# First w_gate chunk issued from the ScalarE queue beside the x tiles; parameter transpose moved into the gate/up work of block 0

## Chip, cores and metric

The kernel runs on one core of a Trainium2 chip. The metric is the device time of one execution in microseconds (us), a median over several runs. The profile's span is shorter than that time by about 1.8 us; all instants below are counted from the span's start.

## The reference

A layer norm of x (2048 rows of 512) feeds two branches that are added to x: a diagonal state-space model over 2048 steps, and a gated feed-forward layer.

```python
xn = _layernorm(x, axis=-1)
return x + _A_ref(xn, Lambda_re, Lambda_im, B_re, B_im, C_re, C_im, log_dt, Dskip) \
         + (_gelu(xn @ w_gate) * (xn @ w_up)) @ w_down      # w_gate, w_up: 512 x 1376
```

## The kernel before

Rows are handled in four blocks of 512. For each block TensorE does the gate and up products (GU), the product of the state-space input matrix with xn (BU), and the down product plus state output (DN). VectorE does the layer norms, the scans and the gelu products; ScalarE does most of the emptying of PSUM, where TensorE's results are written (PS in the profile lines). Every operation is recorded with an estimated duration, its reads and its writes. A list scheduler then picks the order of instructions on VectorE, ScalarE and GpSimd; TensorE and SyncE keep the order of recording. So a small edit can change the order on other engines.

The start of the kernel is what matters here. Cuts are marked.

```python
for j in range(4):
    ld_x0(j)                                  # four x tiles of block 0, SyncE queue
ld_w(WG, WGc, ins["B_w_gate"], 0)             # first chunks: 384 columns each, 384 KB
ld_w(WU, WUc, ins["B_w_up"], 0)
ld_w(WG, WGc, ins["B_w_gate"], 1)
ld_w(WU, WUc, ins["B_w_up"], 1)
for q, nm in enumerate(("A_log_dt", "A_Lambda_re", "A_Lambda_im")):
    S.dma(...PROW..., 1024, ..., queue="scalar")      # three loads of 1 KB, ScalarE queue
# ... cut ...
ACT(lambda e: e.activation(SCR.ap, HALF.ap[:, 0:1], ACTF.Sqrt), 200, [HALF, IOTJ], [SCR], "sqrt0")  # pulls in the Sqrt table
# ... cut: params() transposes the 12 x 128 parameters on TensorE, copies them on VectorE, and computes exp(log_dt) ...

def GU_first(fts, early, single):             # gate/up of block 0, F tiles 0..4; early = 0..2
    # ... cut: mm(ft, u, j0, j1) = 4 matmuls for x tiles j0..j1 (u = 0 gate, 1 up); evac = gelu + copy (ACT), product (V) ...
    for u in range(2):
        for ft in early:
            mm(ft, u, 0, 1)                   # x tile 0
            if single and u == 0 and ft == 1:
                TR0(1, "A")                   # transpose x tile 1, copy it to SBUF on ScalarE
    for ft in early:
        for u in range(2):
            mm(ft, u, 1, 2)                   # x tile 1
        evac(ft, 0)
    late = [ft for ft in fts if ft not in early]
    mm(late[0], 0, 0, 2)
    TR0(2, "V")                               # x tile 2, copied on VectorE
    TR0(3, "A")                               # x tile 3, copied on ScalarE
    for ft in late[1:]:
        mm(ft, 0, 0, 2)
    for ft in late:
        mm(ft, 1, 0, 2)
        evac(ft, 0)
    for ft in fts:                            # the "second half": x tiles 2 and 3
        for u in range(2):
            mm(ft, u, 2, 4)
        evac(ft, 1)

# recording order
PE(fwarm, ...)            # 11 matmuls of 128x512 on zeros, to get TensorE up to speed
LN(0, [0], True)          # layer norm of x tile 0; True: its square root is on ScalarE
TR0(0, "V")
fill(4)
params()
LN(0, [1], True, [GATE["bnag"]])
LN(0, [2, 3], True, [GATE["evT"]])
load_B()
GU_first(range(5), range(3), True)
# ... cut: sine tables, BU(0), the scan of block 0, blocks 1 to 3 ...
```

Of the kernel before, what the change touches and what calls it, by code (L numbers as in the profile page):

```python
# [10 lines left out]
ACTF = mybir.ActivationFunctionType  # L11
# [5 lines left out]
LAT = lambda d, op: SYNC_LAT if d.kind == "dma" or d.eng != op.eng else (0.0 if d.eng == "tensor" else SELF_LAT)  # L17
# [4 lines left out]
class Buf:  # L22
    __slots__ = ("name", "space", "lo", "hi", "ap")

    def __init__(self, name, space, lo, hi, ap=None):
        self.name, self.space, self.lo, self.hi, self.ap = name, space, lo, hi, ap
# [34 lines left out]

class Op:
    __slots__ = ("id", "eng", "fn", "dur", "deps", "kind", "reads", "writes", "start", "finish",
                 "sem", "val", "users", "tag", "issue")

    def __init__(self, id_, eng, fn, dur, kind, reads, writes, tag):
        self.id, self.eng, self.fn, self.dur, self.kind = id_, eng, fn, float(dur), kind
        self.reads, self.writes, self.tag = reads, writes, tag
        self.deps, self.users = [], []
        self.start = self.finish = None  # L70
        self.sem = None
        self.val = None
        self.issue = DMA_ISSUE


class Sched:
# [134 lines left out]
    def _forward(self, prio):  # L211
        ops = self.ops
        free_at = {e: 0.0 for e in ENGINES}
        dma_pipe = 0.0
        ndeps = {op.id: len(op.deps) for op in ops}
        ready = {e: [] for e in ENGINES}
        queue = {e: [op for op in ops if op.eng == e] for e in INORDER}
        qpos = {e: 0 for e in INORDER}
        for op in ops:
            if ndeps[op.id] == 0 and op.eng not in INORDER:  # L220
                ready[op.eng].append(op)
        order = {e: [] for e in ENGINES}
        nleft = len(ops)

        def rdy_time(op):
            return max([d.finish + LAT(d, op) for d in op.deps], default=0.0)

        while nleft:
            best = None
            for e in ENGINES:  # L230
                if e in INORDER:
                    if qpos[e] >= len(queue[e]):
                        continue
                    op = queue[e][qpos[e]]
                    if ndeps[op.id] != 0:
                        continue
                    st = max(free_at[e], rdy_time(op))
                else:
                    if not ready[e]:
                        continue  # L240
                    cands = [(max(free_at[e], rdy_time(op)), op) for op in ready[e]]
                    st0 = min(c[0] for c in cands)
                    stb, b = min(cands, key=lambda c: (prio[c[1].id], c[1].id))
                    if stb <= st0 + 150.0:
                        st, op = stb, b
                    else:
                        limit = max(stb, prio[b.id])
                        fill = [c for c in cands if c[1] is not b and
                                c[0] + (c[1].issue if c[1].kind == "dma" else c[1].dur) <= limit]
                        if fill:  # L250
                            f0 = min(c[0] for c in fill)
                            fill = [c for c in fill if c[0] <= f0 + 150.0]
                            st, op = min(fill, key=lambda c: (prio[c[1].id], c[1].id))
                        else:
                            st, op = stb, b
                if best is None or st < best[0]:
                    best = (st, op)
            st, op = best
            e = op.eng
            if e in INORDER:  # L260
                qpos[e] += 1
            else:
                ready[e].remove(op)
            op.start = st
            if op.kind == "dma":
                free_at[e] = st + op.issue
                xfer = op.dur - 2000.0
                t0 = max(st, dma_pipe)
                dma_pipe = t0 + xfer
                op.finish = t0 + xfer + 2000.0  # L270
            else:
                op.finish = st + op.dur
                free_at[e] = op.finish
            order[e].append(op)
            nleft -= 1
            for u in op.users:
                ndeps[u.id] -= 1
                if ndeps[u.id] == 0 and u.eng not in INORDER:
                    ready[u.eng].append(u)
        return order, max(op.finish for op in ops)  # L280
# [74 lines left out]
def d_dve_tt2x(n): return 100.0 + 0.52 * n  # L355
# [8 lines left out]
def build(nc, ins, out):  # L364
    with ExitStack() as es:
# [11 lines left out]
        WG = A.alloc("WG", [KD, F], BF16)  # L377
# [3 lines left out]
        WGc = [Buf("WGc%d" % i, "sbx", 10 * i, 10 * i + 1) for i in range(3)]  # L381
# [24 lines left out]
        HALF = A.alloc("HALF", [4], F32)  # L406
# [37 lines left out]
        IOTJ = A.alloc("IOTJ", [512], I32, at=OUTB_all.lo)  # L444
# [14 lines left out]
        def ld_w(W, Wc, src, ci, queue="sync"):  # L459
            f0, f1 = FCH[ci]  # L460
            return S.dma(lambda e: e.dma_start(W.ap[:, :, f0:f1], src[:, f0:f1].rearrange("(k p) f -> p k f", p=128)),  # L461
                         512 * (f1 - f0) * 2, writes=[Wc[ci]], tag="ld_w", queue=queue)

        def ld_x0(j):
            S.dma(lambda e, j=j: e.dma_start(X[j].ap, x2[128 * j:128 * (j + 1), :]), 128 * 1024, writes=[X[j]], tag="ld_x0")  # L465
        for j in range(4):
            ld_x0(j)
        ld_w(WG, WGc, ins["B_w_gate"], 0)
        ld_w(WU, WUc, ins["B_w_up"], 0)
        ld_w(WG, WGc, ins["B_w_gate"], 1)  # L470
        ld_w(WU, WUc, ins["B_w_up"], 1)
# [29 lines left out]
        ACT = lambda fn, dur, r, w, tag="", after=(): S.op("scalar", fn, dur, r, w, tag, after)  # L501
# [9 lines left out]
        V(lambda e: e.tensor_scalar(IDN.ap, IOT.ap, 0.0, None, ALU.is_equal), d_dve_ts4x(128), [IOT], [IDN], "ident")  # L511
        POOL(lambda e: e.iota(IOTJ.ap, [[1, 512]], base=0, channel_multiplier=0), 600, [], [IOTJ], "iotj")
        SCR = A.alloc("SCR", [1], F32)
        ACT(lambda e: e.activation(SCR.ap, HALF.ap[:, 0:1], ACTF.Sqrt), 200, [HALF, IOTJ], [SCR], "sqrt0")
        rstate = {"n": 0}

        def next_bank():
# [189 lines left out]
        def GU_first(fts, early, single):  # L707
            banks = [{ft: next_bank() for ft in fts} for h in range(2)]

            def mm(ft, u, j0, j1):  # L710
                W, Wc = ((WG, WGc), (WU, WUc))[u]
                h, q0 = j0 // 2, 256 * u + 128 * (j0 % 2)
                bank = banks[h][ft]

                def f(e):
                    ins_ = None
                    for dk in range(KD):
                        ins_ = e.matmul(PS[bank][:, q0:q0 + 128 * (j1 - j0)], W.ap[:, dk, 128 * ft:128 * (ft + 1)],  # L718
                                        XNT[0].ap[:, dk, 128 * j0:128 * j1], start=(dk == 0), stop=(dk == KD - 1))
                    return ins_  # L720
                PE(f, d_pe([128 * (j1 - j0)] * 4), [Wc[wchunk(ft)]] + XT0[j0:j1], [BANK[bank]], "GU0")

            def evac(ft, h):
                bank, c0 = banks[h][ft], 256 * h
                GATE["nh"] = kk = (GATE["nh"] + 1) % 3
                GATE["last_gelu"] = ACT(lambda e: e.activation(GG[kk].ap[:, 0:256], PS[bank][:, 0:256], ACTF.Gelu_apprx_tanh),
                                        d_act(256), [BANK[bank]], [GG[kk]], "gelu")
                ACT(lambda e: e.activation(UPB[kk].ap[:, 0:256], PS[bank][:, 256:512], ACTF.Copy),
                    d_act(256), [BANK[bank]], [UPB[kk]], "evU")
                V(lambda e: e.tensor_tensor(HTt[0][ft].ap[:, c0:c0 + 256], GG[kk].ap[:, 0:256], UPB[kk].ap[:, 0:256], ALU.mult),  # L730
                  d_dve_tt2x(256), [GG[kk], UPB[kk]], [HTt[0][ft]], "hmul")

            for u in range(2):
                for ft in early:
                    mm(ft, u, 0, 1)
                    if single and u == 0 and ft == 1:
                        TR0(1, "A")
            for ft in early:
                for u in range(2):
                    mm(ft, u, 1, 2)  # L740
# [3 lines that stand above are left out]
            TR0(2, "V")  # L744
            TR0(3, "A")
# [5 lines that stand above are left out]
            for ft in fts:  # L751
# [3 lines that stand above are left out]
# [95 lines left out]
        LN(0, [0], True)  # L850
        TR0(0, "V")
        fill(4)
        params()
        LN(0, [1], True, [GATE["bnag"]])
        LN(0, [2, 3], True, [GATE["evT"]])
        load_B()
# [85 lines left out]
```

## Time and profile before

| | before |
|---|---|
| median of 3 runs at first (6 runs later) | 182.26 us (182.19) |
| span of the profiled run, its time | 180.7 us, 182.48 us |
| matmul busy | 174.4 us, 97% |
| w_gate chunk 0: issued, landed | 2.66, 6.6 |
| w_up chunk 0: issued, landed | 3.13, 8.2 |
| BU of block 0 begins (first weight load) | 16.74 |

Lines of the page of before: span, busy time by engine, and the chain of work that ended last, by engine and by line.

```profile
span 180.7 us, 2411 instructions
...
PE 174.4 (97%) x865; PEld 84.2 (47%) x880; DVE 156.7 (87%) x270; ACT 93.9 (52%) x170; POOL 9.7 (5%) x20
...
PE 93%; DMA 3%; SPq 1%; issue 1%; DVE 0%; DVEq 0%
PE PS L767 37%; PE PS L802 36%; PE PS L655 15%; PE PS L718 5%; DMA arena<-in_B_w_up_dram 3%; SPq L465 1%; DVE arena L818 0%; PE PS L630 0%; SPq L461 0%; DVEq L331 0%
```

TensorE is busy nearly all the time, and the chain is matmuls but for a few per cent at the start. L767 is GU, L802 is DN, L655 is BU, L718 is the gate/up work of block 0 and L630 the x transposes. Next, all waits of TensorE in before: engine, line, what it waited for, us in total, times, longest.

```profile
PE PS L839 <- DVE arena L509: 1.0, 1, 1.0
PE PS L718 <- DVE arena L609: 0.7, 1, 0.7
PE PS L718 <- DMA arena<-in_B_w_up_dram: 0.6, 1, 0.6
PE PS L630 <- DVE arena L609: 0.2, 1, 0.2
```

All four lie in the first 8.3 us. Everything after is an unbroken stream of matmuls, so any gain must come from starting that stream earlier and keeping it whole. The 0.7 us wait, which ends at 6.63, is put down to VectorE's L609, but the copy of x tile 0 that these products need ended at 6.04 (L638, 5.62 + 0.42), and the weight loads ahead of them list 0.80 us for w_gate, which landed at 6.6. The timeline of before for that stretch (start, us, engine, line, operation, output and input, count, then the idle time ahead of it and what ended it; SPq and ACTq are DMA issues):

```profile
1.67 1.28 ACT L514 ACT_TABLE_LOAD   x1 [1.67 <-POOL arena L508]
...
2.66 0.43 SPq L461 DMA_DIRECT2D arena<-in_B_w_gate_dram  x1
...
2.83 0.69 DVE L596 BATCH_NORM_STATS2 arena<-arena 128x6 f32<-128x512 bf16 x1 [0.95 <-DMA arena<-in_A_x_dram]
...
3.13 0.51 SPq L461 DMA_DIRECT2D arena<-in_B_w_up_dram  x1
...
3.86 0.30 ACT L600 ACTIVATE arena<-arena 128x1 bf16<-128x1 bf16 x1 [0.70 <-DVE arena L597]
...
5.19 0.40 PE L630 MATMUL PS<-arena 128*128 128x128 bf16 x4 [0.16 <-DVE arena L609]
...
6.63 0.62 PE L718 MATMUL PS<-arena 128*128 128x128 bf16 x8 [0.71 <-DVE arena L609]
...
8.27 2.62 PE L718 MATMUL PS<-arena 128*128 128x128 bf16 x40 [0.57 <-DMA arena<-in_B_w_up_dram]
...
9.93 0.38 ACT L726 ACTIVATE arena<-PS 128x256 bf16<-128x256 f32 x1
...
11.17 5.84 PE L718 MATMUL PS<-arena 128*128 128x256 bf16 x52
11.37 0.60 ACT L636 ACTIVATE arena<-PS 128x512 bf16<-128x512 bf16 x1 [0.23 <-PE PS L630]
...
16.74 3.23 PEld L655 LDWEIGHTS PS<-arena 128*128 128x128 bf16 x16
```

TensorE: x transpose at 5.19, gate products at 6.63, then a wait for w_up until 8.27. ScalarE: Sqrt table load at 1.67, first layer-norm activation at 3.86, first gelu at 9.93, copy of x tile 3 at 11.37. The start of the second half is not a line of its own, as the 52 matmuls at 11.17 run on without a gap; 12 of them at 0.107 us put it at about 12.45.

The data rate of all DMAs in before, in forty slices of 0.3 us:

```profile
GB/s 0 0 0 0 0 24 208 236 208 252 253 311 259 79 79 125 282 328 346 348 315 294 256 270 270 250 312 294 311 372 393 382 382 386 382 386 382 373 327 256
```

After the x tiles there is a hole of 79 GB/s (3.9 to 4.5 us).

### The profile page before, as it was taken

Reading aid. Unit: us, or ns where it says so; the run is one execution under the profiler, and the core shown is the slowest. Engines: PE = TensorE matmul, PEld = TensorE weight load, DVE = VectorE, ACT = ScalarE, POOL = GpSimd, SP = SyncE. Lnnn points to the kernel's source line nnn. Section 1 sums busy time; section 2 is a strip of 40 time slices with the busy share of each in tenths; the row PEclk is TensorE's granted clock in tenths of the full one; section 3 lists DMA queues with packets and bytes.
Section 4 is the critical chain, followed back from the end, with each engine's and each line's share of the span. In section 5 each row is a group of like instructions: output and inputs, shape, how many; then the busy total and the mean of one; then the engine's idle time right before and its main releaser. Section 6 shows DMA issues by size and latency. Waiting matters only on the chain.

```text
span 180.7 us, 2411 instructions
## 1 busy us (share of the span) xinstructions
PE 174.4 (97%) x865; PEld 84.2 (47%) x880; DVE 156.7 (87%) x270; ACT 93.9 (52%) x170; POOL 9.7 (5%) x20
## 2 busy tenths in 40 slices
PE   7699999999999999999999999999999999999993
PEld 3497444444444444444444444444444444444441
DVE  4779996998989989988999999999989999998111
ACT  4497999876666899002667793000667701700000
POOL 2200112042000000200000000000000000000000
PEclk9999999999999999999999999999999999999999
DMA  5999925999000000002410000000000000003100
GB/s 127 293 326 176 317 46 113 173 314 252 1 0 4 0 0 0 0 31 89 89 29 0 2 0 4 29 29 29 29 0 0 4 0 0 0 0 116 62 29 29
DMA packets 24067, 12.38 MB, mean 68 GB/s; under 512 B 15384, under 2 KB 24056, under 8 KB 24056
## 3 DMA queue, kind: packets, MB, share of 16 engines
q1 hardware_dynamic: 24032, 12.23, 27.5%
q8 instruction: 7, 0.11, 0.3%
q14 instruction: 4, 0.03, 0.1%
q10 hardware_dynamic: 24, 0.00, 0.0%
HBM read 6.46 MB, written 2.10 MB: 47 GB/s over the span
## 4 chain that ended last, share of the span: by engine, by line
PE 93%; DMA 3%; SPq 1%; issue 1%; DVE 0%; DVEq 0%
PE PS L767 37%; PE PS L802 36%; PE PS L655 15%; PE PS L718 5%; DMA arena<-in_B_w_up_dram 3%; SPq L465 1%; DVE arena L818 0%; PE PS L630 0%; SPq L461 0%; DVEq L331 0%
## 5 line engine op out<-in xcount | busy, mean ns | idle before, releaser
L767 PE MATMUL PS<-arena 128*128 128x512 bf16 (+1 forms) x308 | 67.8, 379 | 0.2
L802 PE MATMUL PS<-arena 128*128 128x512 bf16 (+1 forms) x297 | 65.8, 379 | 0.4
L767 PEld LDWEIGHTS PS<-arena 128*128 128x128 bf16 (+1 forms) x312 | 31.4, 100 | 36.1
L779 ACT ACTIVATE arena<-PS 128x512 bf16<-128x512 f32 (+1 forms) x39 | 23.5, 603 | 46.2 <-PE PS L767 36.8
L802 PEld LDWEIGHTS PS<-arena 128*128 128x128 bf16 (+1 forms) x304 | 29.7, 98 | 36.0
L688 DVE TENSOR_TENSOR_SCAN arena<-arena 128x512 bf16<-128x512 f32 x32 | 38.9, 1255 | 0.9 <-POOL arena L536 0.9
L655 PE MATMUL PS<-arena 128*128 128x512 bf16 x124 | 27.7, 379 | 0.2
L782 ACT ACTIVATE arena<-PS 128x512 bf16<-128x512 f32 (+1 forms) x39 | 23.5, 602 | 7.2 <-PE PS L767 7.1
L818 DVE TENSOR_TENSOR arena<-PS,arena 128x512 bf16<-128x512 f32 x16 | 10.6, 681 | 10.7 <-PE PS L802 10.7
L655 PEld LDWEIGHTS PS<-arena 128*128 128x128 bf16 x128 | 12.5, 98 | 14.8
L659 ACT ACTIVATE arena<-PS 128x512 bf16<-128x512 f32 x32 | 17.9, 592 | 2.7 <-PE PS L655 2.6
L784 DVE TENSOR_TENSOR arena<-arena 128x512 bf16<-128x512 bf16 (+1 forms) x39 | 15.5, 414 | 3.6 <-ACT arena L782 3.3
L596 DVE BATCH_NORM_STATS2 arena<-arena 128x6 f32<-128x512 bf16 x16 | 10.3, 682 | 1.4 <-DMA arena<-in_A_x_dram 1.3
L718 PE MATMUL PS<-arena 128*128 128x256 bf16 (+1 forms) x104 | 9.5, 248 | 1.3 <-DVE arena L609 0.7
L794 ACT ACTIVATE PS<-arena 128x512 f32<-128x512 bf16 x16 | 9.4, 602 | 0.7
L677 DVE TENSOR_TENSOR arena<-arena 128x4096 bf16<-128x4096 bf16 (+1 forms) x5 | 9.3, 1856 | 0.0
L675 DVE TENSOR_TENSOR arena<-arena 128x4096 bf16<-128x4096 bf16 (+1 forms) x5 | 9.3, 1855 | 0.0
L700 DVE TENSOR_TENSOR arena<-arena 128x4096 bf16<-128x4096 bf16 x4 | 9.1, 2287 | 0.0
L701 DVE TENSOR_TENSOR arena<-arena 128x4096 bf16<-128x4096 bf16 x4 | 9.1, 2284 | 0.0
L718 PEld LDWEIGHTS PS<-arena 128*128 128x128 bf16 x104 | 8.1, 98 | 2.1 <-DMA arena<-in_B_w_gate_dram 0.8
L609 DVE TENSOR_SCALAR arena<-arena 128x512 bf16<-128x512 bf16 x16 | 5.9, 409 | 0.4
L572 DVE SCALAR_TENSOR_TENSOR arena<-arena 128x512 bf16<-128x512 bf16 x8 | 5.6, 747 | 0.7 <-ACT arena L569 0.7
(81 smaller groups left out, 89.4 us busy)
## 6 DMA issues: line engine op xcount, KB each, us to landing
out_dram<-arena SPq DMA_DIRECT2D x16, 128.0 KB, 1.7
arena<-in_A_x_dram SPq DMA_DIRECT2D x3, 512.0 KB, 7.6
arena<-in_B_w_down_dram SPq DMA_DIRECT2D x1, 1280.0 KB, 7.0
arena<-in_A_x_dram SPq DMA_DIRECT2D x4, 128.0 KB, 2.2
arena<-in_B_w_gate_dram SPq DMA_DIRECT2D x1, 512.0 KB, 5.9
arena<-in_B_w_up_dram SPq DMA_DIRECT2D x1, 512.0 KB, 6.8
arena<-in_B_w_gate_dram SPq DMA_DIRECT2D x1, 480.0 KB, 4.2
arena<-in_B_w_up_dram SPq DMA_DIRECT2D x1, 480.0 KB, 5.1
```

What stands on the lines that cost most here:

```text
L596: V(lambda e, tt=tt: e.bn_stats(ST[tt].ap, X[tt].ap), d_dve_1x(512), [X[tt]], [ST[tt]], "bnst", after)
L655: ins_ = e.matmul(PS[bank][:, :], BBT[c][dk].ap[:, 128 * s:128 * (s + 1)], XNT[b].ap[:, dk, :], start=(dk == 0), stop=(dk == KD - 1))
L659: ACT(lambda e, bank=bank, k3=k3, s=s, c=c: e.activation(SSc[k3][s][c].ap, PS[bank][:, :], ACTF.Copy), d_act(512), [BANK[bank]], [SSc[k3][ ...
L688: V(lambda e, g=g, rb=rb, init=init: e.tensor_tensor_scan(g.ap, rb, g.ap, init, ALU.mult, ALU.add), d_dve_scan(512), [g, PA[RRr]] + ([CARc ...
L718: ins_ = e.matmul(PS[bank][:, q0:q0 + 128 * (j1 - j0)], W.ap[:, dk, 128 * ft:128 * (ft + 1)], XNT[0].ap[:, dk, 128 * j0:128 * j1], start=( ...
L767: ins_ = e.matmul(PS[bank][0:m, c0:c1], W.ap[:, dk, 128 * ft:128 * ft + m], XNT[b].ap[:, dk, c0:c1], start=(dk == 0), stop=(dk == KD - 1))
L779: GATE["last_gelu"] = ACT(lambda e, bg=bg, kk=kk, m=m: e.activation(GG[kk].ap[0:m, :], PS[bg][0:m, :], ACTF.Gelu_apprx_tanh), d_act(512), ...
L782: ACT(lambda e, bu=bu, kk=kk, m=m: e.activation(UPB[kk].ap[0:m, :], PS[bu][0:m, :], ACTF.Copy), d_act(512), [BANK[bu]], [UPB[kk]], "evU")
L784: V(lambda e, kk=kk, m=m, ft=ft, k2=k2: e.tensor_tensor(HTt[k2][ft].ap[0:m, :], GG[kk].ap[0:m, :], UPB[kk].ap[0:m, :], ALU.mult), d_dve_tt ...
L794: ACT(lambda e: e.activation(PS[bank][:, :], X[tt].ap, ACTF.Copy), d_act(512), [X[tt]], [BANK[bank]], "seed")
L802: ins_ = e.matmul(PS[bank][:, :], l_[:, 128 * j:128 * (j + 1)], r_, start=False, stop=last and n == len(ops) - 1, skip_group_check=True)
L818: V(lambda e: e.tensor_tensor(OUTB[ko].ap, PS[bank][:, :], XD[tt].ap, ALU.add), d_dve_1x(512), [BANK[bank], XD[tt]], [OUTB[ko]], "evO")
```

## The change

The intent is to have the first weights arrive sooner, and to keep the parameter transpose from stalling TensorE once its last load sits behind w_gate on ScalarE's queue. `nb` is a "not before" time in the scheduler's model (ns), used only to place an operation in the order of its engine. The table load is thereby put after the DMA issues, and no longer waits for an iota.

```diff
-        ld_w(WG, WGc, ins["B_w_gate"], 0)
+        ld_w(WG, WGc, ins["B_w_gate"], 0, "scalar").nb = 900.0
@@
-        ACT(..., ACTF.Sqrt), 200, [HALF, IOTJ], [SCR], "sqrt0")
+        ACT(..., ACTF.Sqrt), 200, [HALF], [SCR], "sqrt0").nb = 1900.0
@@ rdy_time
-            return max([d.finish + LAT(d, op) for d in op.deps], default=0.0)
+            return max([d.finish + LAT(d, op) for d in op.deps] + [op.nb])
@@ GU_first, between the products of x tile 0 and those of x tile 1
+            params()
@@ recording order
         fill(4)
-        params()
```

(The field `nb` in the class of operations is cut.) Instruction orders that change: ScalarE issues log_dt, Lambda_re, w_gate, Lambda_im and only then loads the Sqrt table; and the scheduler puts one more gelu ahead of the copy of x tile 3. VectorE and GpSimd change in small places.

More of the change, by code (lines that the diff above doesn't have):

```diff
@@ L63 @@
     __slots__ = ("id", "eng", "fn", "dur", "deps", "kind", "reads", "writes", "start", "finish",
-                 "sem", "val", "users", "tag", "issue")
+                 "sem", "val", "users", "tag", "issue", "nb")
     def __init__(self, id_, eng, fn, dur, kind, reads, writes, tag):
@@ L73, in __init__ @@
         self.issue = DMA_ISSUE
+        self.nb = 0.0
 class Sched:
@@ L513, in build @@
         SCR = A.alloc("SCR", [1], F32)
-        ACT(lambda e: e.activation(SCR.ap, HALF.ap[:, 0:1], ACTF.Sqrt), 200, [HALF, IOTJ], [SCR], "sqrt0")
+        ACT(lambda e: e.activation(SCR.ap, HALF.ap[:, 0:1], ACTF.Sqrt), 200, [HALF], [SCR], "sqrt0").nb = 1900.0
         rstate = {"n": 0}
```

## The prediction

> **What bounds the kernel now.** TensorE. The profiled span is 180.7 us, matmuls are busy 174.4 us (97%), the granted clock is full. In the list of waits TensorE waits four times, all before 8.3 us: 1.0 us for the first memset, 0.2 and 0.7 us for layer-norm tiles, 0.6 us for w_up. In the timeline there is no gap over 0.1 us from 8.27 to 177.7 us, so time = start of the unbroken stream + fixed matmul work. The chain of waits agrees: x issues, the w_up chunk (issued 3.13, landed 8.22), then only matmuls.
>
> **What the change does.** (1) The first w_gate chunk (384 KB), issued from SyncE at 2.66 us, landing 3.9 us later, is issued from ScalarE behind two tiny loads that end at 1.58 us. w_up and all behind it on SyncE move up by its issue, 0.47 us. The data rate has a hole now (3.9 to 4.5 us, 80 to 125 GB/s against 250 to 380 around it), which this fills. The Trainium skill, "DMA: Bandwidth & Descriptors", section "Issuing engines are not separate DMA queues", says that such DMAs run on the same 16 engines and interleave, saving only issue time; so I expect no more bandwidth. Estimate: w_gate lands at 5.3 to 5.9 (was 6.6), w_up at 6.7 to 7.3 (was 8.2). (2) The parameter transpose (0.18 us) leaves the gap at 5.74 and goes behind the first up matmuls, about 8.0 us; its copy on VectorE ran only at 7.96, so little is lost. (3) The Sqrt table load (1.28 us) now sits behind four DMA issues on ScalarE: starts near 2.4 instead of 1.67, so the first layer-norm activation goes from 3.86 to about 4.0.
>
> **On the critical path.** First transpose 5.2 to 5.35; its copy done 6.1 to 6.25; gate matmuls start there instead of 6.63; second x transpose waits for its layer-norm tile, about 6.75; third gate tile ends near 7.4; w_up is there. So the stream starts near 7.4, not 8.27: 0.8 us gained. It isn't all kept. The second half of block 0 needs the copy of x tile 3 by ScalarE. Its gelu chain starts at 9.93 because of the layer norm of tiles 2 and 3, which the change doesn't speed up, and the new order puts one more gelu ahead of that copy. Five evacuations at 0.27 us and a 0.60 us copy end near 12.0 us; the second half starts at about 12.45 now (11.17 + 12 x 0.107). So TensorE idles some 0.4 us there, and about 0.4 us is left. Later slack carries it: the first BU matmul is at 16.8 now, its B_re transpose landed at 15.9 and moves up too.
>
> **Prediction.** 181.85 us, range 181.2 to 182.4 (runs of before scatter by 0.7). Faster by over 2%: 0.5%; within 2%: 99%; slower: 0.5%.
>
> **What would show it.** The w_up wait disappears; the 128-column gate/up matmuls run unbroken from near 7.4; a new TensorE wait of 0.2 to 0.5 us near 11.5 to 12 us, released by the ScalarE copy of x tile 3; BU of block 0 starts 0.3 to 0.5 us earlier, everything later is shifted alike; matmul busy time is unchanged.
>
> **What would make it wrong.** w_gate traffic interleaves with x tiles 0 and 1 and delays the first layer norm: no gain or slightly slower. Or the issue on ScalarE takes longer than 0.5 us and pushes the first layer norm beyond 4.1 us. Or the copy of tile 3 isn't the limit and 0.8 us is kept. None reaches 2% (3.6 us): the start-up idle at stake is 1.5 us.

## The result

| | before | after |
|---|---|---|
| median (range), 6 runs each | 182.19 (181.78 to 182.46) | 182.30 (182.25 to 182.75) |
| ratio, 95% interval | | 1.0012 (0.9995 to 1.0028) |
| span and time of the profiled run | 180.7, 182.48 | 180.8, 182.60 |
| w_gate chunk 0 landed | 6.6 | 5.8 |
| w_up chunk 0 landed | 8.2 | 7.35 |
| BU of block 0 begins | 16.74 | 16.84 |

Ratios are the mean time of one kernel's runs over that of the other's of the same rounds, so not quite the ratio of the medians. The change moved the time by less than the comparison can tell from nothing.

The page of after (span, busy, chain by engine):

```profile
span 180.8 us, 2410 instructions
...
PE 175.3 (97%) x865; PEld 84.5 (47%) x880; DVE 156.8 (87%) x270; ACT 93.8 (52%) x170; POOL 9.8 (5%) x20
...
PE 94%; ACT 2%; DVE 2%; issue 1%; DVEq 0%
```

The 2% of ScalarE and 2% of VectorE in the chain are new; DMA has left it. TensorE's waits in after:

```profile
PE PS L841 <- DVE arena L510: 1.0, 1, 1.0
PE PS L719 <- DVE arena L606: 0.4, 1, 0.4
PE PS L719 <- ACT arena L637: 0.3, 1, 0.3
```

The wait for w_up is gone, as intended. A wait for ScalarE's L637 has come in: that is the copy of x tile 3. The timeline of after:

```profile
1.60 0.43 ACTq L462 DMA_DIRECT2D arena<-in_B_w_gate_dram  x1
...
2.51 1.28 ACT L515 ACT_TABLE_LOAD   x1 [2.51 <-issue]
2.65 0.43 SPq L462 DMA_DIRECT2D arena<-in_B_w_up_dram  x1
...
2.94 0.69 DVE L597 BATCH_NORM_STATS2 arena<-arena 128x6 f32<-128x512 bf16 x1 [1.20 <-DMA arena<-in_A_x_dram]
...
4.09 0.30 ACT L601 ACTIVATE arena<-arena 128x1 bf16<-128x1 bf16 x1
...
5.66 0.46 PE L631 MATMUL PS<-arena 128*128 128x128 bf16 x4
...
7.46 1.06 PE L719 MATMUL PS<-arena 128*128 128x128 bf16 x16
...
8.45 0.18 PE L531 MATMUL PS<-arena 12*128 12x12 bf16 x1
...
10.46 0.38 ACT L727 ACTIVATE arena<-PS 128x256 bf16<-128x256 f32 x1
...
11.80 0.64 ACT L637 ACTIVATE arena<-PS 128x512 bf16<-128x512 bf16 x1
...
12.59 4.53 PE L719 MATMUL PS<-arena 128*128 128x256 bf16 x40 [0.32 <-ACT arena L637]
...
16.84 3.23 PEld L656 LDWEIGHTS PS<-arena 128*128 128x128 bf16 x16
```

The loads are issued and land earlier. The up products of x tile 0 begin at 7.69 rather than 8.27. (The line at 7.46 begins with four gate products, 0.056 us apart, which before ran at 7.31, ahead of its wait.) But the first gelu is at 10.46 instead of 9.93. Behind it come five evacuation steps and the copy at 11.80, and TensorE stops for it until 12.59. BU begins 0.1 us later than before. The remaining kernel costs the same: span minus the start of BU is 163.95 and 163.94 us in the two profiles, and the same within 0.03 us in all fourteen. So the start of BU tells all.

The starts of single matmuls in the two traces show where the gain goes. The up products begin 0.58 us earlier (8.27 to 7.69). The parameter transpose takes 0.21 of that: 0.26 us pass from the product ahead of it (8.30) to the one behind it (8.56), where 0.056 is the pace. So the 256-column products begin 0.37 us earlier (11.17 to 10.80). The stop for the copy takes 0.48: 0.59 us pass between two products 0.107 us apart in the stream. (The 0.32 us listed is less, because it counts from the modelled end of the last matmul.) The second half so begins 0.11 us later (12.48 to 12.59), and BU with it.

The data rate in after:

```profile
GB/s 0 0 0 0 0 24 154 254 159 261 102 60 215 369 364 365 377 363 359 378 361 330 298 307 276 287 331 345 386 386 382 386 376 379 372 376 325 246 105 184
```

The hole isn't filled. It has moved forward, to 3.0 to 3.6 us, and the x tiles' landing went from a median of 2.2 to 3.3 us after their issue. The packets in the traces show how: w_gate, issued at 1.60, sends its first packet at 2.87, and from 3.3 to 3.6 us the x tiles (1024 B packets of SyncE's queue) move 3 GB/s and w_gate (768 B packets of ScalarE's) 56. The last packet of the x tiles starts at 5.76 instead of 4.02. Only tile 0 is urgent, and it came at 2.94 against 2.83.

### The profile page after: what moved, and what is told of

Read it like the earlier page. It is cut to its first block, busy times and chain, and to the rows that moved or that the text cites. A ratio compares the mean times of both kernels' runs of the same rounds, so it can differ in the third digit from the quotient of the medians.

```text
span 180.8 us, 2410 instructions
## 1 busy us (share of the span) xinstructions
PE 175.3 (97%) x865; PEld 84.5 (47%) x880; DVE 156.8 (87%) x270; ACT 93.8 (52%) x170; POOL 9.8 (5%) x20
## 4 chain that ended last, share of the span: by engine, by line
PE 94%; ACT 2%; DVE 2%; issue 1%; DVEq 0%
PE PS L769 37%; PE PS L804 36%; PE PS L656 15%; PE PS L841 3%; PE PS L719 3%; ACT L727 1%; DVE arena L597 1%; ACT arena L727 1%; DVE arena L820 0%; ACT arena L729 0%; ACT arena L637 0%; DVE arena L639 0%; DVE arena L610 0%; ACT arena L601 0%; PE PS L631 0%
## 5 line engine op out<-in xcount | busy, mean ns | idle before, releaser
L656 PE MATMUL PS<-arena 128*128 128x512 bf16 x124 | 27.7, 379 | 0.2
L841 PE MATMUL PS<-arena 128*128 128x512 bf16 x11 | 4.9, 632 | 1.0 <-DVE arena L510 1.0
```

The lines of the kernel that those rows point to most:

```text
L656: ins_ = e.matmul(PS[bank][:, :], BBT[c][dk].ap[:, 128 * s:128 * (s + 1)], XNT[b].ap[:, dk, :], start=(dk == 0), stop=(dk == KD - 1))
L841: ins_ = e.matmul(PS[wb][:, :].rearrange("p (a b) -> p a b", a=4), WRM.ap, wrm4, start=True, stop=True)
```

## The experiments

The main theory (A): the gain is turned into a new wait in the second half of block 0, for the copy of x tile 3. A rival (B): the w_gate traffic and the table load behind the DMA issues delay the first layer norm, and that alone eats the gain. Another (C): the moved transpose is the cost. After the first four runs A was widened (A2): the kernel before has variable starts, because the landing of weights and the warm-up of TensorE vary, and its profile was a late one. Twelve programs ran, with 5 or 6 runs each: nine edited kernels, then both kernels unedited and one of the nine again. "Before" is the kernel before on the same chip.

| kernel | median | range | ratio to before (95%) | first gelu | second half begins | BU begins |
|---|---|---|---|---|---|---|
| queue_only | 182.19 | 181.98 to 182.40 | 0.9996 (0.9981 to 1.0010) | 10.37 | 12.21 | 16.47 |
| param_only | 182.29 | 182.06 to 182.73 | 1.0005 (0.9988 to 1.0023) | 10.25 | 12.37 (short stop) | 16.63 |
| copies_first_new | 182.06 | 181.76 to 182.16 | 0.9986 (0.9971 to 1.0000) | 10.12 | no gap | 16.03 |
| copies_first_old | 182.10 | 181.64 to 182.73 | 0.9996 (0.9978 to 1.0014) | 10.56 | no gap | 16.24 |
| warm10_old | 182.13 | 181.88 to 182.62 | 0.9995 (0.9977 to 1.0014) | 10.04 | 11.89 (short stop) | 16.14 |
| warm10_new | 182.31 | 182.24 to 182.45 | 1.0003 (0.9986 to 1.0020) | 10.19 | 12.31 | 16.57 |
| all_new | 181.83 | 181.75 to 182.40 | 0.9982 (0.9964 to 0.9999) | 10.01 | no gap | 16.06 |
| all_old | 182.14 | 181.72 to 182.51 | 0.9992 (0.9974 to 1.0010) | 9.85 | no gap | 16.47 |
| table_first | 182.25 | 181.98 to 182.68 | 1.0005 (0.9985 to 1.0026) | 10.06 | 12.19 | 16.44 |
| after_again | 182.40 | 182.25 to 182.76 | 1.0011 (0.9994 to 1.0029) | 10.43 | 12.55 | 16.81 |
| before_again | 182.39 | 181.82 to 182.49 | 1.0004 (0.9986 to 1.0022) | 10.24 | no gap | 16.60 |
| all_new_again | 181.85 | 181.57 to 181.95 | 0.9978 (0.9961 to 0.9994) | 9.94 | no gap | 15.85 |

The last three columns are from the one profiled run of each. "No gap" means that the second half follows in the unbroken 256-column matmuls. "Short stop" means that the list of waits and the merged timeline show none, but the starts of single matmuls do: 0.15 us are lost in param_only and 0.30 in warm10_old.

### queue_only: the transpose back where it was

```diff
 # changed kernel, in GU_first
-            params()
 # recording order
         fill(4)
+        params()
```

> The changed kernel with the parameter transpose put back before the second layer norm; only the w_gate issue on ScalarE (and the table load's place) is changed. Theory A (the gain of the weights' earlier arrival is taken back because the second half of block 0 waits for ScalarE's copy of x tile 3, which comes after the gelu chain): the scheduler here puts that copy after four evacuations instead of five, so it ends about 0.27 us earlier than in the changed kernel, the TensorE wait before the second half is 0.0 to 0.1 us instead of 0.3, and the time is 181.9 to 182.1 us. Rival B (the w_gate traffic and the table load behind four DMA issues delay the first layer norm by 0.2 us or more and that alone cancels the gain): no difference from the changed kernel, 182.3 us. Rival C (the moved transpose is what costs): also faster, but by the 0.1 us that the transpose takes in the stream. A risk under all: the transpose now waits for Lambda_im, which sits behind w_gate on ScalarE's queue, and stalls TensorE in order.

Measured: 182.19 us. The new wait is 0.24 us. The profile puts it down to VectorE's L538, but it ends 0.14 us after ScalarE's copy (11.44 + 0.63), as it ends 0.15 us after that copy in the changed kernel, so it is read as the same wait. The timeline:

```profile
10.37 0.38 ACT L727 ACTIVATE arena<-PS 128x256 bf16<-128x256 f32 x1
...
11.44 0.63 ACT L637 ACTIVATE arena<-PS 128x512 bf16<-128x512 bf16 x1
...
12.21 4.53 PE L719 MATMUL PS<-arena 128*128 128x256 bf16 x40 [0.24 <-DVE arena L538]
```

Here four evacuation steps stand ahead of the copy instead of five. From first gelu to the second half it takes 1.84 us, against 2.13 in the changed kernel (10.46 to 12.59): 0.29 less, one step. So moving the transpose does cost something, but through the scheduler's new order on ScalarE. Its own 0.21 us in the stream only shortens the wait for the copy that follows. Rival B's "no difference" fails in the trace; the run times (mean 182.15 against 182.41 for the changed kernel) lean the same way without settling it. Theory A's size was off too: the wait fell by 0.08, not by 0.27, as the stream also came earlier.

### param_only: w_gate back on SyncE

```diff
-        ld_w(WG, WGc, ins["B_w_gate"], 0, "scalar").nb = 900.0
+        ld_w(WG, WGc, ins["B_w_gate"], 0)
```

> The changed kernel with w_gate back on the SyncE queue; only the transpose is moved (and the table load sits behind the three small loads). Theory A: w_gate lands at 6.5 and w_up at 8.2 us again, the stream of up matmuls starts at 8.2 to 8.3, the transpose adds 0.1 us to it, so BU of block 0 starts 0.1 us later than in the kernel before; 182.3 us (+0.1). The wait for the copy of x tile 3 is absent, since the stream arrives later. Rival C (the transpose is what costs): slower by more than 0.2 us, 182.5 us or more.

Measured: 182.29 us. A wait for w_gate stands in the list (0.60 us, until 6.73) and none for the copy. But the stream does lose 0.15 us where the second half begins (12.37), 0.14 us after the copy's end (11.59 + 0.64), so the wait wasn't quite absent, against my expectation. w_up landed at 7.7, not at the 8.2 that I expected; that was the first sign that the profile of before was a late case. Rival C's 182.5 us or more did not come (one run of five, 182.73, lies above it).

### copies_first_new and copies_first_old: copies of tiles 2 and 3 ahead of the gelu products, on VectorE

```diff
-                evac(ft, 0)                      # early tiles
@@
             TR0(2, "V")
-            TR0(3, "A")
+            TR0(3, "V")
+            for ft in early:
+                evac(ft, 0, [GATE["evT"]])       # their gelu product comes after the copies
```

The same edit was made on the changed kernel and on the kernel before.

> The changed kernel, with the copy of x tile 3 on VectorE instead of ScalarE, and both copies (tiles 2 and 3) ahead of the first gelu products there. Theory A: the copies end near 11.7 us, before the stream reaches the second half (12.3 us in the changed kernel's profile, 11.9 where the warm-up is not late), the wait of 0.3 us goes, BU of block 0 starts 0.3 to 0.6 us earlier than in the changed kernel, time 181.7 to 182.0. Rival B (the delayed first layer norm is the whole cost): no more than 0.1 us of change, 182.2 to 182.3.

> Control: the same edit of the copies on the kernel before. Theory A: there the copy of tile 3 has 0.4 us of slack, so nothing changes: 182.1 to 182.3, w_up still lands at 8.2 and sets the stream. If this gains as much as the same edit does on the changed kernel, the copy is not what took the gain back but a cost that both kernels have.

Measured: the changed kernel goes to 182.06, with ratio 0.9986 where it had 1.0012 (the intervals overlap slightly); all five runs (up to 182.16) lie below all twelve of the changed kernel (from 182.25). The kernel before with the same edit stays at 0.9996. First the changed kernel's timeline, then the old one's:

```profile
10.44 0.76 DVE L639 COPY arena<-PS 128x512 bf16<-128x512 bf16 x2 [0.31 <-PE PS L631]
10.46 5.84 PE L719 MATMUL PS<-arena 128*128 128x256 bf16 x52
```

```profile
7.56 2.83 PE L718 MATMUL PS<-arena 128*128 128x128 bf16 x44
...
10.68 5.84 PE L718 MATMUL PS<-arena 128*128 128x256 bf16 x52
```

With both copies done by 11.20 (10.44 + 0.76), the 52 matmuls run without a stop; the wait is gone. BU begins at 16.03 instead of 16.84. Of these 0.81 us, 0.34 is an earlier start of the 256-column products, from an early warm-up in this profile (see next), and 0.47 is the stop. So the wait for the copy is a real part of what ate the gain, and the control shows that the edit gives no clear gain on the old kernel. But the old kernel's profile holds a surprise: there is no wait for w_up at all. It landed at 7.6 us, and the 44 products, of which only the fifth and later ones need it, began at 7.56 and never stopped.

### warm10_old and warm10_new: ten warm-up matmuls instead of eleven

```diff
-        nwarm = 11
+        nwarm = 10
```

In the profiles the eleven warm-up matmuls end anywhere between 4.92 us (copies_first_new) and 5.87 us (the changed kernel). The matmul line of the kernel before gives 4.03 us for them and that of the changed kernel 4.88; they start at 0.99 in both. The Trainium skill, "TensorE: Matmul & The Clock Gate", Part 1, says that TensorE begins at half speed, that the window which decides on full speed runs freely, and that the transition therefore varies by ±500 ns from run to run. Traces show more: in their clock records the full clock is granted at 3.82 us in copies_first_new and at 6.00 in copies_first_old, 2.2 us apart, with the other kernels in between (two traces hold no record). Where it comes after the eleventh matmul, as in the changed kernel (5.81), all eleven run at the slow pace, and the first x transpose waits behind them.

> The kernel before with 10 warm-up matmuls instead of 11. In the profiles so far the moment when TensorE speeds up lies anywhere between 4.0 and 5.5 us; at the slow pace (0.427 us each) 11 warm-up matmuls end at 5.69, 10 end at 5.26, while the first normalized x tile is ready at 5.13 here. Theory A2 (in the kernel before the stream waits for whichever is last, the layer-norm chain or w_up, which lands anywhere between 7.6 and 8.2 us): a late warm-up is mostly hidden here behind w_up, so little is gained, 182.0 to 182.2 us. Rival D (the warm-up is the whole spread, w_up is not): 181.8 us and no run above 182.1.

> The changed kernel with 10 warm-up matmuls. Its first normalized tile is ready at 5.34, after the warm-up's latest end of 5.26, so the warm-up can't hold it any more. Theory A2 (in the changed kernel nothing hides a late warm-up: it delays the layer norm of tiles 2 and 3, hence the gelu chain on ScalarE and the copy of tile 3): the spread of its runs shrinks and the time falls by 0.2 to 0.3 us against the changed kernel, to 182.0 us; the wait for the copy of tile 3 stays, 0.3 us. Rival B (the load traffic and the table load's place are the whole loss): unchanged, 182.2 to 182.3 us.

Measured: 182.13 and 182.31 us. (The 3.82 to 6.00 us of the clock records is wider than the 4.0 to 5.5 of my expectation.) The changed kernel's spread shrinks from 182.25 to 182.76 (12 runs) to 182.24 to 182.45, and its slower cluster (five of the twelve runs, from 182.55 on) doesn't appear in six runs. But the median doesn't fall; the other seven of the twelve were at 182.3 already. The timeline of warm10_new:

```profile
10.19 0.38 ACT L727 ACTIVATE arena<-PS 128x256 bf16<-128x256 f32 x1
...
11.52 0.65 ACT L637 ACTIVATE arena<-PS 128x512 bf16<-128x512 bf16 x1
...
12.31 4.53 PE L719 MATMUL PS<-arena 128*128 128x256 bf16 x40 [0.32 <-ACT arena L637]
```

The first gelu is 0.27 us earlier than in the changed kernel's profile (10.46), and so is the second half (12.59 to 12.31). The wait is still 0.32. So the late warm-up explains the late profile and probably the slower cluster of the changed kernel, not its usual time. For the kernel before, 182.13 fits A2; rival D ("no run above 182.1") is refuted by runs up to 182.62. The profile of warm10_old holds something the list of waits hides. w_up landed early there (7.2), and then the copy of x tile 3 stops the kernel before too:

```profile
10.21 6.20 PE L718 MATMUL PS<-arena 128*128 128x256 bf16 x52
...
11.12 0.63 ACT L636 ACTIVATE arena<-PS 128x512 bf16<-128x512 bf16 x1
```

The 52 products take 6.20 us where 5.84 is the unbroken time. Most of the rest is one stop of 0.30 us before the second half, which begins at 11.89, 0.14 us after the copy's end. So the copy is the next limit in both kernels. All five profiles that have the new load order and leave the copy on ScalarE wait for it. With the old load order and order of recording (before, before_again, warm10_old) only the one whose loads land early does.

### table_first: Sqrt table load ahead of the w_gate issue

```diff
-        ACT(..., "sqrt0").nb = 1900.0
+        ACT(..., "sqrt0")
```

ScalarE's order becomes log_dt, table load, Lambda_re, w_gate, Lambda_im.

> The changed kernel with the Sqrt table load ahead of the last two small loads and the w_gate issue on ScalarE; nothing else. Theory A2: the first layer-norm activation starts at 3.95 instead of 4.09, the gelu chain at about 10.05 where the warm-up is not late (10.19), the copy of tile 3 ends at 12.03, the wait for it shrinks from 0.32 only to about 0.2 us, and the time is 182.1 to 182.2 us. Rival B (the table load's place is the whole loss): 181.8 to 181.9 us, like the version with all three edits.

Measured: 182.25 us, not clearly different from before or from the changed kernel. The timeline:

```profile
2.97 0.69 DVE L597 BATCH_NORM_STATS2 arena<-arena 128x6 f32<-128x512 bf16 x1 [1.24 <-DMA arena<-in_A_x_dram]
...
4.00 0.30 ACT L601 ACTIVATE arena<-arena 128x1 bf16<-128x1 bf16 x1 [1.18 <-DVE arena L598]
...
12.19 4.53 PE L719 MATMUL PS<-arena 128*128 128x256 bf16 x40 [0.32 <-ACT arena L637]
```

From the first statistics instruction to the first layer-norm activation it takes 1.03 us here, as in before (2.83 to 3.86). In the changed kernel it is 1.15 (2.94 to 4.09), in warm10_new 1.29. So the table load's place costs 0.1 to 0.3 us of the layer-norm chain. In all five profiles with the load behind the DMA issues (it starts at 2.49 to 2.51) that activation comes at 4.08 to 4.10, though x tile 0 came anywhere from 2.81 to 2.94: there the load sets the instant, not the tile. Rival B as the whole loss is refuted: the wait for the copy is still 0.32, and the time isn't 181.8. My expectation that the wait would shrink was wrong too. The stream and the gelu chain both hang on the first layer norm, so a delay of it moves them together and leaves the wait between them as it was.

### all_new and all_old: hindrances taken away together

all_new is the changed kernel with copies first, ten warm-up matmuls and the early table load; all_old is the kernel before with copies first and ten warm-up matmuls (its table load is early).

> The changed kernel with the copies of tiles 2 and 3 first on VectorE, 10 warm-up matmuls, and the Sqrt table load ahead of the w_gate issue on ScalarE. Each of the three hindrances named so far is taken away. Theory A2: first layer-norm activation at 3.95 instead of 4.09, second half without a wait, BU of block 0 starts at 15.9 to 16.1 us (16.84 in the changed kernel's profile), 181.6 to 181.8 us, faster than both kernels in every run's median. If it stays at 182.0 or more, a further limit that I don't know sits in the first 16 us.

> The kernel before with the same copies first and 10 warm-up matmuls (its table load is early already); w_gate on SyncE and the parameter transpose where it was. What it is slower than all_new by is what the change is worth once its own hindrances are gone. Theory A2: w_up lands between 7.6 and 8.2 us and becomes the limit in most runs; 181.8 to 182.1, 0.2 to 0.4 us slower than all_new. Rival E (the earlier w_gate is worth nothing, since the layer norms decide): equal to all_new within 0.1 us.

Measured: 181.83 and 182.14 us. In all_old TensorE waited 0.36 us for w_up, which landed at 7.9; in all_new the list of waits has none, and the starts of the matmuls show a loss of 0.13 us when it landed at 7.3. The difference of the medians, 0.3 us, is what the change seems worth once nothing behind it takes the gain back; the two intervals overlap, so the size is loose. all_new is 0.03 us above the expected range. Against its expectation, one of its runs (182.40) lies among the slow runs of before.

### after_again, before_again, all_new_again: all three on one chip

The first two are unedited; the third is all_new again.

> The changed kernel itself, unedited, on the same chip as the others of this call. Theory A2: 182.25 to 182.35 in most runs, 182.6 to 182.75 where the warm-up is late; the wait for the copy of tile 3 is there again at 0.3 us; w_up lands at 7.0 to 7.5 us. If the wait is absent, it was an accident of one profile.

> The kernel before itself, as a control: it shows how far equal kernels differ in this comparison (ratio 1.000, interval within 0.2%), and gives a second sample of where w_up lands. Theory A2: its landing scatters between 7.2 and 8.2 us, the one profile of before (8.22) was at the late end; so the w_up wait is likely to be smaller than 0.57 us here. If it lands at 8.2 again, the profile was typical and the baseline was not the error.

> The changed kernel with all three edits again, on the same chip as the unedited two: 181.8 to 181.95 us, 0.3 to 0.5 us below the changed kernel and 0.3 to 0.4 below the kernel before. If it isn't below both, the first result for it was the chip's.

Measured: 182.40, 182.39 and 181.85 us. The control of before against itself gives 1.0004 (0.9986 to 1.0022), so a ratio of 1.0012 is within what equal kernels show. The changed kernel has its 0.32 us wait again, and no run of 12 under 182.25, while before reaches down to 181.71. In before_again w_up landed at 8.1, late once more, and w_gate at 7.0:

```profile
PE PS L718 <- DMA arena<-in_B_w_gate_dram: 1.0, 1, 1.0
```

```profile
7.04 0.62 PE L718 MATMUL PS<-arena 128*128 128x128 bf16 x8 [1.02 <-DMA arena<-in_B_w_gate_dram]
...
7.72 3.03 PE L718 MATMUL PS<-arena 128*128 128x128 bf16 x44
```

This time the listed wait is for w_gate (1.02 us). The 44 products from 7.72 take 3.03 us, against 2.83 in copies_first_old, so w_up cost 0.2 us at most there. Its landing wasn't an early one, against my expectation, but it cost less. By the test that I had set ("if it lands at 8.2 again, the profile was typical"), the late landing is usual for the kernel before, of which there are only these two profiles. Over six profiles with the old load order w_up landed at 8.2, 7.7, 7.6, 7.2, 7.9 and 8.1; over eight with the new one at 7.0 to 7.5.

all_new_again ran the block without a stop:

```profile
10.28 5.84 PE L719 MATMUL PS<-arena 128*128 128x256 bf16 x52
```

It is 0.22% faster than before (0.9978, interval 0.9961 to 0.9994) and 0.3% below the changed kernel's median. Its slowest run (181.95) is below the fastest of the changed kernel (182.25). It is the best version found, and beats both.

## Why the prediction was right or wrong

The range (181.2 to 182.4) holds the time and "within 2%" was right. But the range also covers no gain at all (before is at 182.19), so that it held the time says nothing for the mechanism. The forecast of a 0.4 us gain was wrong: none came.

**Right.** The wait for w_up disappeared. w_gate landed at 5.8 (forecast 5.3 to 5.9) and w_up at 7.35 (6.7 to 7.3, so just outside). A new wait for ScalarE's copy of x tile 3 appeared, 0.32 us (forecast 0.2 to 0.5). The order on ScalarE, five evacuation steps and the copy, took 1.98 us from first gelu to the copy's end (10.46 to 11.80 + 0.64), as summed.

**The step that failed: "Its gelu chain starts at 9.93 because of the layer norm of tiles 2 and 3, which the change doesn't speed up".** I took 9.93 over unchanged into the sum. It measured 10.46. By the program's order the layer norm of tiles 2 and 3 follows VectorE's copy of the transposed tile 0, so it hangs on the first layer norm and on TensorE. That copy came at 6.16 instead of 5.62.

The change slows this chain: the first layer-norm activation came at 4.09 instead of 3.86, 0.23 us later. That is where the table load behind four DMA issues puts it, whenever x tile 0 arrives (five profiles, 4.08 to 4.10). With the load early it would have come 1.03 us after the statistics, at 3.97 (an estimate from before and table_first), 0.12 earlier. The 0.11 that would be left is the arrival of x tile 0 (2.94 against 2.83), which scatters from 2.75 to 2.97 over both load orders and so isn't shown to come from the change. My own text had "about 4.0" for this activation, and the sum left it out. The remaining 0.3 us is the late warm-up of that run: the first transpose ran at 5.66, although its tile was ready at 5.34. warm10_new, without it, has 10.19.

Hence the second half began at 12.31 to 12.59, not at 12.0. Besides, 0.15 us passes from the end of the copy to the first matmul in the changed kernel (12.44 to 12.59), which the sum also left out. The stop costs the stream 0.48 us, where the prediction had 0.4.

**The gain ahead of it was smaller too: "0.8 us gained".** It measured 0.58 at the up products, because the first gate products began at 6.73 and not at 6.1 to 6.25 (the same late chain: the copy of x tile 0 ended at 6.58). The transpose then took 0.21 us of it, where the prediction had "little is lost". In warm10_new, without the late warm-up, the up products begin at 7.41, which is 0.86 earlier than in before.

**The baseline: "the second half starts at about 12.45 now".** That is one profile, whose run took 182.48 us, while before has a median of 182.2 to 182.4 in five samples. With the old load order BU begins earlier where w_up lands earlier: 16.74 (w_up at 8.2), 16.60 (8.1), 16.47 (7.9), 16.24 (7.6) and 16.14 (7.2), only the first two of them of the kernel before itself; param_only, with the transpose in the stream, has 16.63 (7.7). Against before_again's 16.60 almost nothing is left of the changed kernel's gain without a late warm-up (16.57 in warm10_new). The wait for w_up that the change removes is thus not a fixed 0.57 us: four of the six profiles with the old load order list none. But two of these four list a wait for w_gate instead (1.02 and 0.60 us) and lose another 0.15 to 0.2 us on w_up.

**Wrong as well.** "Which this fills": the hole in the data rate moved forward and wasn't filled. "BU of block 0 starts 0.3 to 0.5 us earlier": it started 0.1 later. Matmul busy time rose by 0.9 us (174.4 to 175.3), nearly all of it the warm-up (4.03 to 4.88), and wasn't unchanged. Why w_gate's issue takes over a microsecond to become traffic (1.60 to 2.87, against 2.66 to 3.77 before), and why the x tiles nearly stop at that point, was not tried and stays open.

Where did the gain go, then? By the traces the change traded a start that depends on when loads land (runs of before: 181.7 to 182.7) for one held by the layer-norm and gelu chain (after: never below 182.25). The fastest runs of before have no profile, so what makes them fast is not shown. That the wait for the copy is part of it is shown by copies_first_new and its control. The parts of the layer-norm delay are read from traces; in run time alone, table_first and warm10_new are too near to before to be told apart.

## What to carry to other kernels

Before costing the removal of a DMA wait, look at more than one profile: a wait on a load at the start can be 0.6 us in one profile and absent in the next. Look at the starts of single instructions too: a merged line without a listed wait hid stops of up to 0.3 us here. When a start-up wait is removed, list every other chain that meets the same stream a few microseconds later, and price how the change moves that chain too, including what it puts ahead of it in the engine's issue order. With a list scheduler, compare instruction orders on all engines, and test an edit meant to take a wait away on the old kernel as well.

## What the Trainium skill lacked or had wrong

- "DMA: Bandwidth & Descriptors", section "Issuing engines are not separate DMA queues", says that issuing from several engines only saves the sequencer's time, usually small next to the DMA. No run here shows more bandwidth: the highest slice of the two rows above is 393 GB/s before and 386 after. What the section lacks is a size for that time and what it delays on the issuing engine: w_gate's issue took 0.43 us on ScalarE, the 1 KB load behind it 0.42 us instead of 0.26, and the table load began at 2.51 instead of 1.67.
- The same page gives no run-to-run scatter of landing times. The same 384 KB load, w_up with the old load order, landed 4.1 to 5.1 us after its issue in six profiles.
- "TensorE: Matmul & The Clock Gate", Part 1, gives ±500 ns of variation of the transition, which is too little for these runs (full clock granted between 3.82 and 6.00 us, with the first matmul at 0.98 to 0.99 in all). Its remark in the same Part that one kernel ran 6, 11 or 14 slow matmuls fits better: here it is seven to all eleven of the warm-up. It calls the penalty under 1% of a typical span; here too it is 0.3 us of 182, but that is the size of the whole effect under test.
- "ScalarE: Activation LUTs", section "What ACT_TABLE_LOAD costs", gives 1283 ns for the load, as here (1.28 us), and about 1380 ns of drain besides. No such drain shows here: in before the load runs from 8.63 to 9.91 right behind a Sqrt that ends at 8.61, and the first gelu starts at 9.93, 1.32 us after the Sqrt's end in all.
